# Reworking the front of a fused attention and feed-forward kernel: loads, masks, and the order of the first feed-forward pass

## The chip, the cores and the metric

The kernel runs on one core of one Trainium2 chip. The metric is the device time of one execution in microseconds (us), as a median over several executions. The core has five engines that work side by side (in the kernel before, TensorE is busy for 97% of the span, VectorE for 58, ScalarE for 43 and GpSimd for 24): TensorE (PE in the profile), VectorE (DVE), ScalarE (ACT), GpSimd (POOL) and SyncE (SP), besides 16 DMA engines. "Granted clock" is the TensorE clock that the chip allowed, as a share of full speed; the trace records when it changed. "Span" is the time from the first to the last instruction of the profiled execution, about 1.7 us less than the device time.

## The reference, cut to what matters

```python
# q, k, v: (8 batches, 8 heads, 576 rows, 64) float32
scores = scale * np.matmul(q, k.transpose(0, 1, 3, 2))
mask_plain = (rel >= 0) & (rel < 32)                           # heads 0 to 3
mask_dil = (rel >= 0) & (rel < 128) & (rel % 4 == 0)           # heads 4 to 7
scores = np.where(masks, scores, -1e9)
...                                                            # softmax over the row
attn_out = np.matmul(attn, v)
x = attn_out.transpose(0, 2, 1, 3).reshape(8 * 576, 512)
g = x @ w_gate                                                 # 512 x 1536
out = (gelu(g) * (x @ w_val)) @ w_out                          # 4608 x 512
```

## The kernel before

Heads are worked on in pairs. A batch has four pairs: 0 and 1 with the plain mask, 2 and 3 with the dilated one. The finished pair n goes to tile `xT[n]` (128 features by tokens, float16), and the feed-forward part contracts over these four tiles. The "front" is batch 0's attention, after which the first chunk of 512 tokens can enter the feed-forward part; the attention of later batches is woven into it.

The front, with cuts (`...`). Filler matmuls (`warm`) keep TensorE at work during the first loads. `gate["dma"]` and `gated` make the next load wait until an earlier one has landed.

```python
for t, src, eng in ((0, q, nc.sync), (1, k, nc.scalar)):
    eng.dma_start(out=first_p[:, t], in_=sixes(src, 0))      # both plain pairs, float32
qd0 = load_eights(0)                                         # dilated q, k: cast DMA on GpSimd
...
identity(); mask_plain(); mask_dil()                         # GpSimd selects over whole masks
gate_v = v_plain(0, sv0, nc.sync)
nc.sync.dma_start(out=fh(first_vd), in_=quads(v, 0, HK, 0, 4 * P))   # dilated v, float32
warm(24, 7)
...                                                          # casts, transposes of pairs 0 and 1
gate["dma"] = gate_v
load_w_halves(0)                                             # first third of gate and value weights
v_cast(0, sv0)
emit_s(0, 4, pe_mask=True)                                   # scores and exponentials of pair 0
emit_s(1, 0, pe_mask=True)
t_dil(0, 0, qd0, 4, ("dve", "dve"))
...
w1 = load_w(1)[1]                                            # second third
...
den(3, 4)
norm_x(2, 2)                                                 # xT of pair 2, on DVE
num(3, 0)                                                    # xT of pair 3, on DVE
load_w(2)
gate["dma"] = w1                                             # batch 1's q, k wait for the second third
for t, src in ((0, q), (1, k)):
    gated(nc.sync.dma_start(out=st1[:, t], in_=sixes(src, 1)))
```

The first two feed-forward blocks take the four `xT` tiles one after the other, each tile for all four accumulations before the next, so that TensorE can start with the tile that is ready first:

```python
def ffn1_two(c, pairs, order, split):
    kcs = parts_of(order)
    for group in [kcs[:-1], kcs[-1:]] if split else [[kc] for kc in kcs]:
        for nb in range(2):
            for gi in range(2):
                ffn1_part(c, nb, gi, pairs[nb][gi], group)
...
ffn1_two(c, ..., range(NKC), False)                          # order 0, 1, 2, 3
```

The softmax here doesn't subtract the row's maximum and nothing guards it: scores larger than these inputs give would overflow.

## Time and profile before

| What | Before |
|---|---|
| device time, median of 3 runs | 348.39 us (348.38 to 348.97) |
| span of the profiled execution | 347.0 us |
| TensorE busy | 336.0 us, 97% |
| granted clock | 1.0 throughout the work |
| first feed-forward matmul | 20.97 us |
| its first two blocks done | 25.29 us |
| last transposes for batch 1 start | 43.56 us |
| next feed-forward part starts | 62.06 us |

The lines behind these numbers stand in the prediction. A timeline line reads: start, length, engine, source line, operation, destination and sources by the program's names, shapes, count, and in brackets the idle time of the engine before it with what ended it. The place that absorbs most is the wait for batch 1's k at 41.57.

### The profile page before, as it was taken

To read this page: it belongs to the slowest core of one execution; us is meant where nothing else is said; L and a number is where in the kernel's file an instruction comes from. 1 tells how busy PE (TensorE), PEld (TensorE's weight loads), DVE (VectorE), ACT (ScalarE), POOL (GpSimd) and SP (SyncE) were. 2 spreads that over 40 slices of the span, in tenths; PEclk is the share of its full clock that TensorE was granted. 3 is DMA by queue.
4 is the path that set the end of the run, shared out by engine and by line. 5 is a ranking of instruction groups with operands and counts; after the bars stand their busy time and mean duration, and the time that the engine had idled before them with its cause. 6 is when DMAs were issued, how large, how long until landed. Compare 5 with 4: busy or idle time off the path is not lost.

```text
span 347.0 us, 6006 instructions
## 1 busy us (share of the span) xinstructions
PE 336.0 (97%) x2342; PEld 163.7 (47%) x2342; DVE 201.8 (58%) x309; ACT 148.2 (43%) x220; POOL 84.0 (24%) x123
## 2 busy tenths in 40 slices
PE   8879999999999999999999999999999999999996
PEld 3644454444544445444544454444444444444443
DVE  3784488443794359674878576975498423303320
ACT  1753473535543447336553547336633223223321
POOL 8893304630630540351006300510000000000000
PEclk9999999999999999999999999999999999999999
DMA  8999999999999999898169925991100020020002
GB/s 179 225 201 223 205 200 192 184 147 258 178 107 256 191 152 171 201 162 121 62 159 168 157 73 137 195 126 55 70 0 0 32 91 1 2 91 30 2 30 91
DMA packets 107516, 44.44 MB, mean 128 GB/s; under 512 B 83328, under 2 KB 102912, under 8 KB 107488
## 3 DMA queue, kind: packets, MB, share of 16 engines
q1 hardware_dynamic: 84192, 31.01, 39.2%
q0 software_dynamic: 22752, 12.33, 28.9%
q10 hardware_dynamic: 544, 0.72, 0.8%
q8 instruction: 18, 0.29, 0.4%
q14 instruction: 10, 0.08, 0.1%
HBM read 39.85 MB, written 9.44 MB: 142 GB/s over the span
## 4 chain that ended last, share of the span: by engine, by line
PE 70%; DVE 13%; DMA 10%; issue 3%; ACT 2%; SPq 1%; POOL 1%; DVEq 0%; POOLq 0%; ACTq 0%
PE ps L584 42%; PE ps L618 21%; PE ps L472 4%; DMA st<-in_k_dram 4%; DMA sv<-in_v_dram 3%; DMA wv<-in_moe_w_val_dram 3%; DVE dt L500 2%; DVE dt L533 2%; DVE u_all L607 2%; DVE xT L559 2%; DVE rb L544 2%; DVE P L400 2%; DVE xT L510 1%; PE ps L390 1%; DVE rc L542 1%
## 5 line engine op out<-in xcount | busy, mean ns | idle before, releaser
L607 DVE SCALAR_TENSOR_TENSOR u_all<-g,ps 128x512 f16<-128x512 f16 x108 | 72.8, 684 | 76.7 <-PE ps L584 67.9
L606 ACT ACTIVATE g<-ps 128x512 f16<-128x512 f32 x108 | 63.9, 596 | 123.3 <-PE ps L584 122.8
L584 PE MATMUL ps<-xT,wg 128*128 128x512 f16 x432 | 114.0, 379 | 1.2 <-POOL xT L707 0.7
L584 PE MATMUL ps<-xT,wv 128*128 128x512 f16 x432 | 113.8, 379 | 0.2 <-DVE u_all L607 0.2
L618 PE MATMUL ps<-wo,u_all 128*128 128x512 f16 x420 | 96.9, 380 | 0.2 <-DVE qTd L303 0.2
L584 PEld LDWEIGHTS <-wv 128*128 128x128 f16 x432 | 42.2, 98 | 52.8 <-issue 2.9
L584 PEld LDWEIGHTS <-wg 128*128 128x128 f16 x432 | 41.3, 98 | 48.9 <-issue 1.1
L618 PEld LDWEIGHTS <-u_all 128*128 128x128 f16 x420 | 38.4, 98 | 44.7 <-issue 0.8
L629 ACT ACTIVATE osb<-ps 128x512 f32<-128x512 f32 x33 | 19.7, 597 | 38.8 <-PE ps L618 37.8
L228 POOL CAST qp<-st 128x2048 f16<-128x2048 f32 x6 | 11.4, 1893 | 97.8 <-DMA st<-in_k_dram 64.8
L544 DVE STREAM_TRANSPOSE rb<-rc 128x576 f32<-128x576 f32 (+4 forms) x34 | 25.3, 743 | 1.3
L533 DVE STREAM_TRANSPOSE dt<-ps 128x576 f32<-128x576 f32 x21 | 16.3, 778 | 12.4 <-PE ps L472 12.3
L392 ACT ACTIVATE P<-ps 128x1152 f16<-128x1152 f32 x16 | 18.1, 1130 | 11.8 <-PE ps L390 11.8
L370 ACT ACTIVATE P<-ps 128x960 f16<-128x960 f32 x16 | 15.5, 970 | 11.0 <-PE ps L360 11.0
L559 DVE TENSOR_TENSOR xT<-ps,rb 128x576 f16<-128x576 f32 x16 | 17.9, 1129 | 2.2 <-PE ps L472 1.9
L400 DVE TENSOR_TENSOR P<-P,mask_d 128x1152 f16<-128x1152 f16 x13 | 9.8, 751 | 9.7 <-ACT P L392 9.7
L400 DVE TENSOR_TENSOR P<-P,mask_p 128x1344 f16<-128x1344 f16 x14 | 11.8, 856 | 2.9 <-ACT P L371 2.9
L472 PE MATMUL ps<-P,ones 128*64 128x96 f16 (+5 forms) x174 | 11.3, 244 | 2.1 <-DVE P L400 1.5
L472 PEld LDWEIGHTS <-ones 128*64 128x64 f16 x174 | 7.2, 109 | 11.5 <-issue 8.6
L631 DVE TENSOR_SCALAR osb<-ps 128x512 f32<-128x512 f32 x2 | 1.4, 691 | 18.2 <-PE ps L618 18.2
L255 POOL DMA_DIRECT2D vr<-in_v_dram x16 | 9.9, 632 | 5.3 <-DMA wv<-in_moe_w_val_dram 3.6
L500 DVE STREAM_TRANSPOSE dt<-ps 64x576 f32<-64x576 f32 x14 | 10.9, 781 | 0.4
(88 smaller groups left out, 247.8 us busy)
## 6 DMA issues: line engine op xcount, KB each, us to landing
out_dram<-osb SPq DMA_DIRECT2D x35, 256.0 KB, 2.0
sv<-in_v_dram SPq DMA_DIRECT2D x40, 128.0 KB, 3.3
st<-in_q_dram SPq DMA_DIRECT2D x24, 128.0 KB, 3.1
st<-in_k_dram SPq DMA_DIRECT2D x24, 128.0 KB, 3.1
vd<-in_v_dram POOLq DMA_DIRECT2D x7, 256.0 KB, 6.5
wo<-in_moe_w_out_dram POOLq DMA_DIRECT2D x3, 512.0 KB, 19.7
qd<-in_q_dram POOLq DMA_DIRECT2D x6, 256.0 KB, 5.4
qd<-in_k_dram POOLq DMA_DIRECT2D x6, 256.0 KB, 6.9
```

The costliest lines, as they stand in the source:

```text
L392: nc.scalar.activation(pt, ps[:, b0 : b0 + 4, 0:DW], AF.Exp, bias=0.0, scale=scale)
L400: nc.vector.tensor_tensor(pt, pt, mb, ALU.mult)
L472: nc.tensor.matmul(o, lhs, rhs, start=st, stop=True, skip_group_check=True)
L500: nc.vector.transpose(dt[64 * hl : 64 * hl + 64].rearrange("p b c -> p (b c)"), both_rows(1 - hl, b0, hl))
L533: nc.vector.transpose(dst, den)
L544: nc.vector.transpose(rb[:, 0 : 32 * nb].rearrange("p (b c) -> p b c", c=32), bass.AP(tensor=rc.tensor, offset=rc.offset, ap=[rc.ap[0], [1 ...
L559: nc.vector.tensor_tensor(dst.rearrange("p (i m s) -> p i m s", m=2, s=2), num, rb.rearrange("p (s m i) -> p i m s", s=2, m=2), ALU.mult,)
L584: nc.tensor.matmul(ps[:, bank, :], w[:, kc, ns], xT[kc][:, tok], start=first, stop=end)
L606: nc.scalar.activation(g, ps[:, banks[0], :], AF.Gelu)
L607: nc.vector.scalar_tensor_tensor(u_all[:, nb, :], g, USCALE, ps[:, banks[1], :], ALU.mult, ALU.mult)
L618: nc.tensor.matmul(ps[:, bank, :], u_all[:, fc, tb * P : (tb + 1) * P], wo_t[fc // 4][:, fc % 4, :], start=(fc == 0), stop=(fc == NNB - 1),)
L629: nc.scalar.activation(osb, ps[:, bank, :], AF.Copy, bias=0.0, scale=1.0 / USCALE)
```

## The change

It is meant to shorten the front. Of the plain pairs' q and k, only the first pair's are still loaded as float32; the second pair's and the dilated v come by DMAs that cast (they convert float32 to float16 on the way), issued from GpSimd. One block of each mask is built by GpSimd and the rest copied from it by VectorE. The scores of pair 0 run at once, with VectorE masking them. The fillers fall from 24 to 18, and the first feed-forward pass takes the tiles in the order 2, 0, 1, 3. The core of the diff, with cuts:

```diff
+    def copies(n, w):
+        return bass.AP(tensor=mask_p.tensor, offset=mask_p.offset, ap=[mask_p.ap[0], [0, n], [1, w]])
+    def mask_copies():
+        nc.vector.tensor_copy(mask_p[:, PW:PB].rearrange("p (r c) -> p r c", c=PW), copies(2, PW))
+        nc.vector.tensor_copy(mask_p[:, PB : PB + P], mask_p[:, 0:P])
+        nc.vector.tensor_copy(by_class[:, :, 0:P], copies(2, P))
...
-        eng.dma_start(out=first_p[:, t], in_=sixes(src, 0))
+        eng.dma_start(out=first_p[:, t], in_=sixes(src, 0)[:, 0:2])
+    for t, src in ((0, q), (1, k)):
+        nc.gpsimd.dma_start(out=q6b[:, t], in_=sixes(src, 0)[:, 2:4])
+    identity()
     qd0 = load_eights(0)
+    band(run_p.rearrange("p (r c) -> p r c", r=1), 0, 0)
+    band(rest_p.rearrange("p (r c) -> p r c", r=1), 0, 64)
     sv0 = new_v(0)
-    load_v_dil_rest(0)
-    identity()
-    mask_plain()
-    mask_dil()
+    load_v_dil(0)
+    band(rest_d, 64, 48)
...
-    warm(24, 7)
+    warm(11, 7)
+    for t in range(2):
+        cast_six(("dve", "act")[t], q6a, first_p, t, 0)
+    t_plain(0, q6a, 0, 0, ("act", "dve"))
+    warm(3, 3)
+    mask0 = emit_s(0, 4)
+    mask_copies()
+    warm(4, 3)
...
-    emit_s(0, 4, pe_mask=True)
     emit_s(1, 0, pe_mask=True)
-    t_dil(0, 0, qd0, 4, ("dve", "dve"))
-    t_dil(0, 1, qd0, 6, ("act", "act"))
+    den(0, 2)
+    t_dil(0, 0, qd0, 6, ("act", "act"))
+    t_dil(0, 1, qd0, 2, ("dve", "dve"))
...
-                ffn1_two(c, ((4, 5), (6, 7)) if c == 0 else ((6, 7), (0, 1)), range(NKC), False)
+                ffn1_two(c, *((((4, 5), (6, 7)), (2, 0, 1, 3)) if c == 0 else (((6, 7), (0, 1)), range(NKC))), False)
```

## The prediction

> **What bounds the kernel now.** I read the busy shares first, then the timeline of TensorE, then the chain of waits of the first 45 us, then the DMA throughput of the same stretch, and at last the DMA packets that the trace records.

> ```profile
> PE 336.0 (97%) x2342; PEld 163.7 (47%) x2342; DVE 201.8 (58%) x309; ACT 148.2 (43%) x220; POOL 84.0 (24%) x123
> ```

> TensorE has work in 97% of the span, so a change that leaves its work after the front alone gains only what it takes off the start. The timeline of TensorE in the first 45 us (start, length, line, count, idle before and its releaser):

> ```profile
> 1.53 7.51 PE L658 MATMUL ps<-ones 128*128 128x512 f16 x24 [1.53 <-DVE ones L66]
> 8.88 1.26 PE L314 MATMUL ps<-ident,qp 96*128 96x96 f16 x24
> ...
> 13.40 0.95 PE L332 MATMUL ps<-ident,qd 72*128 72x72 f16 x24 [0.82 <-ACT P L370]
> ...
> 20.97 0.38 PE L584 MATMUL ps<-xT,wg 128*128 128x512 f16 x1 [0.37 <-POOL xT L707]
> ...
> 41.57 0.43 PE L314 MATMUL ps<-ident,qp 96*128 96x96 f16 x6 [0.32 <-POOL qp L301]
> ```

> The front (batch 0's attention) lasts until the feed-forward part starts at 20.97. From 25.29 on, the four groups of the first two blocks done, TensorE runs dense up to 40.83; there it transposes batch 1's q, waits 0.32 us for batch 1's k, and from then on is dense to the end: no later idle in the timeline is over 0.41 us. So whatever the front gains must pass the wait at 41.57. What stands behind it, in the chain of waits of this stretch (start, length, what):

> ```profile
> 3.88 11.30 DMA sv<-in_v_dram
> ...
> 17.74 9.37 DMA wv<-in_moe_w_val_dram
> ...
> 27.55 13.09 DMA st<-in_k_dram
> 40.64 0.05 issue
> 40.69 0.83 POOL qp L301
> 41.52 0.05 issue
> 41.57 0.43 PE ps L314 x6
> ```

> It is a chain of transfers, not of engine work: v of batch 0, then the second third of the gate and value weights (wv lands at 17.74 + 9.37 = 27.11), then batch 1's q and k, which are held back until those weights land, then a cast on GpSimd. Are the transfers late because they are issued late, or because the DMA engines are full? Throughput of 16 to 27 us (40 equal slices):

> ```profile
> DMA  9999999999999999999999999999999999999999
> GB/s 201 205 194 197 246 186 184 184 196 194 194 194 199 199 196 203 201 205 205 201 214 205 201 216 197 209 205 201 205 212 205 209 209 209 197 220 194 209 201 216
> DMA packets 3138, 2.23 MB, mean 203 GB/s; under 512 B 95, under 2 KB 3137, under 8 KB 3137
> ```

> Full throughout. These are cast transfers, counted at their float16 output; 203 GB/s out is about 406 GB/s of float32 read. The packets say the same of the whole start: from 1.75 us on there is no gap, and the last packet of the second weight third starts at about 25.75 us. Up to there the DMA engines move batch 0's q, k, v (3 x 1.18 MB of float32, plus 0.33 MB read twice) and four weight pieces of 1.05 MB: 8.06 MB in 24.0 us, 336 GB/s. **The DMA engines bound the first 41 us; TensorE bounds the rest.**

> [...]while two queues are active, they start packets about one for one (36 cast packets of 1024 B and 36 of 256 B per 0.25 us near 9.5 us). So moving loads from SyncE's queue to GpSimd's buys no bandwidth. [...]The 24 filler matmuls fit: 7.51 us = 11 x 0.427 + 13 x 0.216, the switch at about 6 us. [...]the kTr copy of 128x256 takes 228 ns on DVE and 401 ns on POOL.

> **The change part by part.**

> *First pair of q, k.* Before, 2 x 576 KB of float32 land at 0.81 + 6.9 = 7.7 and 0.81 + 7.5 = 8.3 us. Now half of it. In the packets, the first 384 of the 768 of these loads had started by 4.5 us, and landing trails by about 1 us: 5.4 to 5.8. Cast on DVE 0.58 and on ACT 0.83, 12 transposes 0.6, copies 0.75, 3 fillers 0.65, scores 0.47: scores of pair 0 end near 8.3 (before: 11.1) and its exponentials (0.97 + 0.48) near 9.8 (before 12.5). A gain of 2.7 us for pair 0 alone.

> *Second pair, dilated q, k.* [...]second pair (384 packets), then dilated q, k (576), then v. The first packet of this queue starts at 6.7 us in the trace though it was issued at 1.40, and I take the same start. From there 384 cast packets of 1536 B read (about 61 ns of one engine each, scaled from 80 ns for 2048 B) are 1.5 us, 576 x 80 / 16 = 2.9 us, and the rest of v's 256 B packets beside them 1.3 us: done near 12.4, dilated k landed near 13.5. Before: 2.29 + 11.1 = 13.4. No gain: the dilated pairs still wait for the same bytes.

> *Masks.* POOL's selects and memsets before the weights (0.88 + 0.66 + 2.99 + 0.73 + 1.33 = 6.6 us, from 4.24 to 10.95) shrink to about 2.8 (2 x 0.29 identity, 2 x 0.36 run, 2 x 0.55 rest, 2 x 0.21 dilated rest), with four short memsets and three copies, 0.4 + 0.7 us, on DVE while it is idle (it waited 4.18 us). The weights are issued from about 9.5 instead of 10.97. The DMA engines are full then, so earlier issue alone moves nothing.

> *v dilated as a cast DMA.* 512 KB on SyncE and a POOL cast of 1.07 us go; the same bytes come by GpSimd's queue. TensorE had waited 0.44 us for that cast, but not on the bounding chain.

> *Denominator of pair 0 before the dilated part.* Takes 0.75 + 0.22 + 0.78 = 1.75 us of DVE out of the crowded stretch after 13.5. DVE then has there: copies 1.5, kTr 0.23, three denominators of 1.8, two products of 1.06: 9.3 us from about 14.3, so the last xT group at about 23.6 against 24.4. TensorE takes 0.86 us per group and now starts with xT of pair 2, which I put near 22.5; with that order the first two blocks end between 24.5 and 26 (before 25.29).

> *The sum.* Two times decide, and the later wins. TensorE's own arrival at batch 1's k: 40.83 + 0.42 before, now shifted by -0.8 to +0.6. Batch 1's k: same bytes ahead of it. What gets cheaper is the 384 float32 packets of the second pair: in the trace they ran at 96 to 107 ns instead of 65 ns (from 4.25 us to about 7), some 2.4 us net of the v packets; as casts 1.5 us. Estimate from these: 0.75 us earlier at best, 0 if the slow spell is due to something else. So the cast that TensorE waits for ends 0 to 0.8 us earlier, and after it nothing changes. TensorE's arrival may take part of that back. Expected gain: 0.5 us, so 348.39 - 0.5 = 347.9 us.

> **The rivals.**

> 1. *The whole front gain reaches the end.* If the dilated loads also land earlier (GpSimd's queue starting at 4 us, not 6.7), the feed-forward part could start up to 2 us earlier, and the time would be 346.4. For it: TensorE, DVE and POOL all lose work in the front. Against: the full DMA engines; the second weight third landed at 27.11 for a use at 28.7 to 29.6, a slack of about 2 us, but batch 1's k has none. It would need that k to land 2 us earlier too, at the same byte count.

> 2. *The new order costs.* [...]v's cast has to wait for v, and the kTr copy of pair 2 and the second weight third's issue stand behind it. If v lands at 15.5 instead of 13, pair 2's scores slip by 1.5 to 2 us, the feed-forward part starts later than now, and the time becomes about 349.5. For it: before, v landed at 15.18 and DVE, not POOL, copied these keys. Against: v is now behind only half as much on SyncE's queue, and its 2560 small packets have the engines nearly to themselves from 4.5 to 6.7 us.

> 3. *The clock drops.* Fillers fall from 24 to 18 and TensorE idles between 9 and 14 us for the second pair and the dilated k. [...] Before shows a granted clock of 1.00 in every stretch and idles under 0.9 us.

> **Range and chances.** From rival 1, weighted low, to the cost of rivals 2 and 3 in part: 346.5 to 349.0, which also covers the run-to-run spread of 348.38 to 348.97. Two per cent is 7 us, a third of the whole front; with the DMA engines full that is out of reach, and nothing added costs as much. Faster 0.01, same 0.975, slower 0.015.

> **What would show it.** Scores of pair 0 near 8 us instead of 10.6; dilated transposes still held until about 13.5; DMA at 9 in all slices to 41 us; the second weight third landing between 26 and 27.3; and a longer TensorE wait for the k cast (up to 1.2 us instead of 0.32) if the feed-forward part starts earlier. I am wrong if batch 1's k lands over 1 us earlier or later than 40.64, or if the first two feed-forward blocks end after 26.5. Predicted time: 347.9 us, 346.5 to 349.0.

## The result, and the profile after

The changed kernel took 351.43 us (median of 4 runs, 350.99 to 351.58) against 348.63 us (348.38 to 348.97, 4 runs) of the kernel before in the same rounds. Ratios here are the mean time of one kernel's fast runs over that of the other's of the same rounds, so not quite the ratio of the medians quoted: 1.0078, with a 95% interval of 1.006 to 1.0095. By the 2% rule that is "same", yet it is 2.8 us slower and lies above the predicted range of 346.5 to 349.0. What separates them is the granted clock: 0.995 in all four runs after, 1.0 in the profiled run before, and 0.998 to 1.0 in the runs of the kernel before in all later rounds.

The busy line of the page after:

```profile
PE 335.6 (96%) x2344; PEld 163.2 (47%) x2344; DVE 203.9 (58%) x315; ACT 148.4 (42%) x220; POOL 82.6 (24%) x118
```

TensorE has as much work as before and the span is 2.8 us longer: idle time was added. The timeline of TensorE after, in the front, answers to the one in the prediction:

```profile
7.63 0.47 PE L364 MATMUL ps<-qTp 64*128 64x160 f16 x10 [0.20 <-DVE qTp L297]
...
13.08 0.95 PE L336 MATMUL ps<-ident,qd 72*128 72x72 f16 x24 [1.17 <-DMA qd<-in_k_dram]
...
22.66 0.38 PE L588 MATMUL ps<-xT,wg 128*128 128x512 f16 x1 [2.41 <-DVE xT L563]
22.87 0.42 PE L588 MATMUL ps<-xT,wv 128*128 128x512 f16 x1
23.09 0.63 PE L588 MATMUL ps<-xT,wg 128*128 128x512 f16 x1
...
26.07 0.59 PE L588 MATMUL ps<-xT,wv 128*128 128x512 f16 x1
26.50 0.38 PE L588 MATMUL ps<-xT,wg 128*128 128x512 f16 x1
...
27.79 1.03 PE L588 MATMUL ps<-xT,wg 128*128 128x512 f16 x4
...
43.33 0.68 PE L318 MATMUL ps<-ident,qp 96*128 96x96 f16 x12
```

The scores of pair 0 start at 7.63 instead of 10.64, and the dilated transposes at 13.08 instead of 13.40: the early part works as meant. Then three things stand in the next lines. TensorE waits 2.41 us, for the tile of pair 2. From 23.09 on each matmul takes 0.63 us instead of 0.38 and starts 0.43 us after the last instead of 0.21. And the first two blocks end at 27.79 instead of 25.29. At 43.33 all twelve transposes of batch 1's first pair run as one group, so the wait at 41.57 that bounded the kernel before is gone.

Were the other tiles ready? The timelines of VectorE and GpSimd after, at that time:

```profile
21.52 2.12 DVE L563 TENSOR_TENSOR xT<-ps,rb 128x576 f16<-128x576 f32 x2
```

```profile
19.13 2.76 POOL L719 TENSOR_TENSOR xT<-xT,rb 128x576 f16<-128x576 f32 x2 [3.05 <-ACT xT L718]
```

GpSimd writes `xT` of pairs 0 and 1, done at about 20.5 and 21.9. VectorE writes those of pairs 2 and 3, the first done at about 22.6. The order 2, 0, 1, 3 asks for the one that comes third.

```profile
19.66:23.07 3.41, 0.88 (x14) 0.62 (x14) 3.27 (x6) 1.35 (x2) 3.41 (x4) 1.00 1.24 205
23.07:26.48 3.41, 3.41 (x9) 1.21 (x8) 0.57 (x1) 0.00 (x0) 3.41 (x6) 0.50 1.13 174
```

```profile
19.66:23.07 3.41, 2.71 (x36) 1.66 (x37) 2.92 (x5) 1.46 (x2) 3.41 (x4) 1.00 1.31 204
23.07:26.48 3.41, 3.35 (x16) 1.36 (x14) 2.31 (x4) 1.21 (x3) 3.41 (x5) 1.00 1.24 206
```

In the window before the fall TensorE worked 0.88 us in the changed kernel and 2.71 in the kernel before. The window after it ran at half clock: 9 matmuls instead of 16 for the same full 3.4 us. Half of 3.41 us, 1.7 us, is lost.

The chain of waits after (start, length, what) no longer runs through batch 1's k:

```profile
4.25 8.79 DMA qd<-in_k_dram
...
20.82 0.78 DVE rb L548
21.59 1.02 DVE xT L563
22.62 0.04 issue
22.66 20.84 PE ps L588 x88
```

It goes from the dilated k through VectorE's work on the denominators to the tile of pair 2, and from there on it is TensorE. Before, DMA made up 10% of the chain and now 3%.

A last difference lies in the next stage. The last transposes for batch 1 start at 45.58 (before 43.56, so 2.02 later), but the next feed-forward part starts at 64.93 (before 62.06, 2.87 later): the stage took 19.35 us instead of 18.50. VectorE, GpSimd and TensorE after:

```profile
51.23 1.72 DVE L404 TENSOR_TENSOR P<-P,mask_p 128x1344 f16<-128x1344 f16 x1 [0.81 <-ACT P L375]
...
51.21 1.04 POOL L206 CAST vp<-sv 128x1024 f16<-128x1024 f32 x1 [9.62 <-DMA sv<-in_v_dram]
...
56.22 0.44 PE L476 MATMUL ps<-P,ones 128*64 128x288 f16 x4 [0.70 <-DVE dt L537]
```

and the same product and cast before:

```profile
49.23 0.86 DVE L400 TENSOR_TENSOR P<-P,mask_p 128x1344 f16<-128x1344 f16 x1 [0.66 <-ACT P L371]
...
52.49 1.04 POOL L212 CAST vp<-sv 128x1024 f16<-128x1024 f32 x1 [9.43 <-DMA sv<-in_v_dram]
```

This product of scores and mask takes 0.86 us by itself and 1.72 us where it starts 0.02 us after a GpSimd cast, and TensorE waits 0.70 us for what follows it.

### The profile page after: what moved, and what is told of

Same layout as the page of the kernel before. It is cut to its first block, busy times and chain, and to the rows that moved or that the text cites. A ratio compares the mean times of both kernels' runs of the same rounds, so it can differ in the third digit from the quotient of the medians.

```text
span 349.8 us, 6009 instructions
## 1 busy us (share of the span) xinstructions
PE 335.6 (96%) x2344; PEld 163.2 (47%) x2344; DVE 203.9 (58%) x315; ACT 148.4 (42%) x220; POOL 82.6 (24%) x118
## 4 chain that ended last, share of the span: by engine, by line
PE 76%; DVE 15%; issue 3%; DMA 3%; ACT 2%; POOL 1%; DVEq 0%; POOLq 0%; ACTq 0%
PE ps L588 48%; PE ps L622 21%; PE ps L476 4%; DMA qd<-in_k_dram 3%; DVE dt L537 2%; DVE rb L548 2%; DVE xT L563 2%; DVE dt L504 2%; DVE P L404 2%; DVE u_all L611 2%; DVE xT L514 1%; PE ps L394 1%; DVE rc L546 1%; PE ps L364 1%; PE ps L646 1%
## 5 line engine op out<-in xcount | busy, mean ns | idle before, releaser
L548 DVE STREAM_TRANSPOSE rb<-rc 128x576 f32<-128x576 f32 (+4 forms) x34 | 25.3, 743 | 1.3
L537 DVE STREAM_TRANSPOSE dt<-ps 128x576 f32<-128x576 f32 x23 | 17.9, 779 | 12.6 <-PE ps L476 12.5
L374 ACT ACTIVATE P<-ps 128x960 f16<-128x960 f32 x16 | 15.5, 970 | 12.2 <-PE ps L364 12.1
L404 DVE TENSOR_TENSOR P<-P,mask_p 128x1344 f16<-128x1344 f16 x15 | 13.5, 912 | 3.2 <-ACT P L375 3.2
```

The costliest lines, as they stand in the source:

```text
L404: nc.vector.tensor_tensor(pt, pt, mb, ALU.mult)
L537: nc.vector.transpose(dst, den)
L548: nc.vector.transpose(rb[:, 0 : 32 * nb].rearrange("p (b c) -> p b c", c=32), bass.AP(tensor=rc.tensor, offset=rc.offset, ap=[rc.ap[0], [1 ...
```

## The experiments

The theory: the order makes TensorE wait for pair 2, and the wait leaves too little TensorE work in one window of 3.41 us (0.88 us in after, 2.71 in before), so the clock halves for the next. Rivals: the wait alone costs the time; the front's new loads and masks cost it; the collision of VectorE and GpSimd costs it. Runs called "undisturbed" have a granted clock of 0.998 or more.

### The order and the clock

**e1_order0123**: the changed kernel with the old order.

```diff
-                ffn1_two(c, *((((4, 5), (6, 7)), (2, 0, 1, 3)) if c == 0 else (((6, 7), (0, 1)), range(NKC))), False)
+                ffn1_two(c, ((4, 5), (6, 7)) if c == 0 else ((6, 7), (0, 1)), range(NKC), False)
```

> The changed kernel with the old order (0, 1, 2, 3) of the first two feed-forward blocks, nothing else. Theory A (the order 2, 0, 1, 3 makes TensorE wait 2.4 us for xT of pair 2, and that wait drops the clock): groups start near 20.6, 22.0, 22.7 and 23.7, the two blocks end near 24.6 instead of 27.8, the granted clock stays at 1.0, the DVE mask product near 50 us takes 0.86 us again, and the time is 1.0 to 1.5 us under the kernel before (ratio 0.996 to 0.997). Theory B (fewer fillers or the long wait for the dilated q, k drop the clock): the clock still falls to 0.5 for 3.4 us near 23 us, and at least 1.7 us of the loss stays (ratio 1.003 or more).

Measured: 347.45 us (6 runs), before 348.81; ratio 0.9978 (0.9948 to 1.0007). Five runs lie between 347.31 and 347.63 at clock 1.0 (mean 347.44), one at 350.98 with clock 0.985. TensorE's timeline:

```profile
20.43 0.38 PE L588 MATMUL ps<-xT,wg 128*128 128x512 f16 x1 [0.35 <-POOL xT L719]
...
21.79 0.38 PE L588 MATMUL ps<-xT,wg 128*128 128x512 f16 x1 [0.34 <-POOL xT L719]
...
24.40 1.03 PE L588 MATMUL ps<-xT,wg 128*128 128x512 f16 x4
```

The first block starts at 20.43 with short waits and both end at 24.40, 0.89 us earlier than before and 3.39 us earlier than after. Everything else in the change makes the kernel faster by about 1.4 us when the clock holds; over all six runs the interval still includes 1. One run in six shows that the clock does not always hold.

**e4_before2013**: the kernel before with the new order, and nothing else (the same line exchanged the other way).

> The kernel before with only the order 2, 0, 1, 3 taken over. Theory A: TensorE waits from about 20.5 to 23.4 for xT of pair 2, the clock falls for 3.4 us at about 23.0, the two blocks end near 28.3 instead of 25.3; the wait for batch 1's k (0.32 us) goes; time 2.3 to 3.0 us over the kernel before (ratio 1.0065 to 1.0085), so the order alone makes the whole loss. Theory B (the loads or the masks make it): ratio under 1.003.

Measured: 351.22 us (5 runs), ratio 1.0066 (1.0053 to 1.0079), clock 0.994 or 0.995 in all five. The timeline:

```profile
23.57 0.58 PE L584 MATMUL ps<-xT,wg 128*128 128x512 f16 x1 [2.80 <-DVE xT L559]
...
28.67 1.03 PE L584 MATMUL ps<-xT,wg 128*128 128x512 f16 x4
```

A wait of 2.80 us, a fall of the clock at 23.53 for 3.41 us, and a loss of 2.4 us, without any other part of the change. The order by itself is enough for a loss of this size.

**e2_fill11** and **e3_fill4**: the changed kernel, order kept, with filler matmuls in the wait, to part the wait from the clock.

```diff
     num(3, 0)
+    warm(11, 4)          # e2; e3 has warm(4, 4)
```

> The changed kernel with order 2, 0, 1, 3 kept and 11 filler matmuls put before the first feed-forward matmul. Theory A: the wait for xT of pair 2 stays (first matmul near 22.7), but the clock is held, so the two blocks end near 26.1 instead of 27.8; the DVE mask product near 50 us no longer meets GpSimd's cast of v, so 0.85 us more comes back: time 0 to 0.6 us over the kernel before (ratio 1.000 to 1.002). If the clock is not the matter but only the wait, the time stays at 1.006 to 1.009.

> As with 11 fillers, but only 4 (0.86 us of work): asks how much work in a 3.41 us stretch holds the clock. TensorE then works some 1.7 of the 3.41 us before 23.07, against 0.9 in the changed kernel and 2.7 in the kernel before. If about half is enough, the clock stays at 1.0 and the time is that with 11 fillers; if not, it is that of the changed kernel (ratio about 1.008).

Measured: e2 349.18 us (6 runs), ratio 1.003 (0.9998 to 1.0062). Its five undisturbed runs have a mean of 349.21; one run, the profiled one, took 353.07 with a clock that fell at 13.15 already. e3 349.97 us (4 runs), ratio 1.0042 (1.0019 to 1.0064), three undisturbed at 349.36 to 350.30, the profiled one at 351.74 with a fall at 14.37. So with four fillers the clock held at 23 in these four runs. With the clock held, the order still costs 349.21 - 347.44 = 1.8 us, the wait itself; against the changed kernel's 351.43, from other rounds, what the fillers bring back is about 2.2 us, of which 1.7 is the halved window. Why e3 is half a microsecond over e2 stays open. The undisturbed runs of e2 and e3 have no profile of their own.

### The collision on VectorE

**e5_vcast_act**: batch 1's v cast on ScalarE instead of GpSimd; for room, the output buffers were cut from four to two.

```diff
-    osbp = ctx.enter_context(tc.tile_pool(name="osbp", bufs=4))
+    osbp = ctx.enter_context(tc.tile_pool(name="osbp", bufs=2))
...
-    v_cast(1, sv1)
...
+            v_cast_act(1, sv1)
```

> The changed kernel with batch 1's cast of v taken from GpSimd and given to ScalarE at a later place (the v staging gets two buffers and the output staging two instead of four to make room). Theory A2 (the DVE mask product of 1.72 us at 51.2 was blocked by that cast, and was on the path): the product takes 0.86 us, and the time falls by 0.7 to 0.9 us against the changed kernel, to about 350.6 (ratio to the kernel before about 1.0055). Rival: the product is slow for another reason, or its delay is hidden: it stays at 1.7 us, or the time stays within 0.2 us of the changed kernel (ratio about 1.008).

Measured: 368.1 us (4 runs), ratio 1.0557. A failed design, as TensorE's timeline shows:

```profile
79.45 0.58 PE L596 MATMUL ps<-xT,wg 128*128 128x512 f16 x1 [15.08 <-ACT osb L641]
```

With two output buffers ScalarE waited 21.42 us for the stores, and TensorE 15.08 us for ScalarE. The product did take 0.86 us, but the time says nothing of the collision.

**e5b_vcast_act**: the same cast on ScalarE, the staging buffer put into columns of `xT` that are not used yet, so that the output buffers stay at four.

```diff
-    sv1 = new_v(1)
+    sv1 = x32[2][:, 0 : 5 * HK * D].rearrange("p (k h d) -> p k h d", k=5, h=HK)
+    tiles["v", 1] = vset[1]
-    v_cast(1, sv1)
...
+            v_cast_act(1, sv1)
```

> The experiment on batch 1's cast of v again, without its fault: the first try took two output buffers away, and TensorE then stood 15 us behind the stores. Now only the v staging of batch 1 lies elsewhere (in columns of xT that are not yet in use), and the cast is on ScalarE at a later place. Theory A2: the DVE mask product near 51 us takes 0.86 us instead of 1.72, TensorE's idles before 54 and 56 us shrink by about 0.85 us in sum, and the time is 350.6, 0.7 to 0.9 us under the changed kernel (ratio to the kernel before 1.0045 to 1.006). Rival: the delay of the product is made up elsewhere; the ratio stays at 1.007 to 1.008.

Measured: 352.42 us (6 runs), ratio 1.0116 (1.0093 to 1.014). The product takes 0.86 us and the stage 18.49 (18.50 in before), and yet the time is no lower. In the profiled run the clock fell twice, at 13.24 for 10.24 us and at 26.90 for 3.41 us, and no run was undisturbed. Inconclusive on the time.

**f1_after_fill** and **f2_after_fill_vcast**: the changed kernel with five fillers in the wait for the dilated k (all 11 runs of e8 and f4, below, are undisturbed with them), without and with the cast on ScalarE.

```diff
-    def t_dil(b, hp, q8, b0, engs):
+    def t_dil(b, hp, q8, b0, engs, fill=0):
...
+            if t and fill:
+                warm(fill, b0 + t)
...
-    t_dil(0, 0, qd0, 6, ("act", "act"))
+    t_dil(0, 0, qd0, 6, ("act", "act"), fill=5)
```

> The changed kernel, order 2, 0, 1, 3 kept, with only the 5 fillers in the wait for the dilated k. The drop at 13 or 14 us does not come (no clock under 0.993), the one at about 23 us still does (clock 0.994 to 0.996), time 351.0 to 351.6, ratio 1.007 to 1.009.

> The same with batch 1's cast of v moved from GpSimd to ScalarE. If the stage from the last transposes of batch 1's q, k to the next feed-forward part takes 19.35 us in most runs of the changed kernel, as in its profiled one, and 18.49 without the cast, this is 0.7 to 0.9 us under the kernel with fillers only, at about 350.5 (ratio 1.0050 to 1.0065). If the collision is the accident of single runs, or the order's loss would have grown otherwise, the two are equal within 0.3 us.

Measured: f1 351.82 us (6 runs), ratio 1.0076 (1.0054 to 1.0097); f2 352.18 us (6 runs), ratio 1.0096 (1.0073 to 1.0118). Moving the cast gains nothing here. The clocks were partly missed as well: two runs of each were at 0.989 or 0.99, and one of f1 held 1.0 throughout. That one took 349.78 us; the three of f1 at 0.995 have a mean of 351.47, 1.7 us more, in the same kernel and rounds. The traces show why the cast is not worth its 0.85 us. In f1 the product at 51 us starts just before the cast, and the cast is the one that takes longer, 1.71 instead of 1.04 us; but a later product collides. VectorE, GpSimd and TensorE of f1:

```profile
87.45 2.27 DVE L406 TENSOR_TENSOR P<-P,mask_d 128x1152 f16<-128x1152 f16 x1 [1.45 <-ACT P L398]
...
87.22 1.89 POOL L222 CAST qp<-st 128x2048 f16<-128x2048 f32 x1 [12.57 <-DMA st<-in_k_dram]
...
89.77 0.44 PE L478 MATMUL ps<-P,ones 128*64 128x192 f16 x8 [0.86 <-DVE P L406]
```

This product takes 0.72 us by itself. f2, whose first collision was removed, has the same one there (2.41 us, TensorE idle for 1.00), and so has e2 (2.18 us, idle 0.76). A kernel whose start moved has its products elsewhere against GpSimd's casts, and which of them meet is a matter of that run. None of the profiled runs of before, e1, e3, e4, e6 to e10, f4 and g1 has a product over 0.88 us. Where one is stretched in the stage from batch 1's last transposes, the stage grows with it: 19.35 us in after (1.72 us), 19.36 in f3 (1.58), 18.93 in g2 and g3 (1.15 and 1.29), against 18.48 to 18.58 in all other profiles. From there to the end e2, f1 and f2 take 286.0 to 286.6 us, and all others but e5 284.8 to 285.3. So a collision does cost time in the run that has it. In the profiles f2 had nothing to save in this stage: f1 had no stretched product there either (18.49 us in both), and both lost 1.1 to 1.7 us later.

### Where the front's gain comes from

The prediction said that issuing the weights earlier moves nothing. In e1 SyncE issues batch 1's q at 25.29 us, in before at 27.17. These runs put single parts of the change into the kernel before.

**e6_before_qk**: the second pair's q and k by cast DMA.

```diff
-        eng.dma_start(out=first_p[:, t], in_=sixes(src, 0))
+        eng.dma_start(out=first_p[:, t], in_=sixes(src, 0)[:, 0:2])
+    for t, src in ((0, q), (1, k)):
+        nc.gpsimd.dma_start(out=q6b[:, t], in_=sixes(src, 0)[:, 2:4])
...
```

> The kernel before with only the second pair's q, k as cast DMA on GpSimd's queue. Batch 1's k was issued 1.6 us earlier in the changed kernel (25.6 instead of 27.2). If that came from these 384 float32 packets, which ran slowly (96 to 107 ns each), the second third of the weights lands 1.0 to 1.6 us earlier here; if it came from v or from the shorter work on GpSimd, under 0.5 us. The end: TensorE's wait for batch 1's k shortens, at most 0.3 us, ratio 0.997 to 1.001.

Measured: 348.74 us (4 runs), ratio 1.0003 (0.9987 to 1.002). Batch 1's q is issued at 27.20: no earlier. The expectation missed.

**e7_before_vcastdma**: the dilated v by cast DMA.

```diff
-    load_v_dil_rest(0)
+    load_v_dil(0)
...
-    nc.sync.dma_start(out=fh(first_vd), in_=quads(v, 0, HK, 0, 4 * P))
-    copy("pool", tiles["v", 0][1], r4(first_vd))
```

> The kernel before with only the dilated v as cast DMA (no float32 copy, no cast on GpSimd). If v were the reason why the weights land earlier, they land over 1 us earlier here; I expect under 0.5 us, since the same bytes are read. The second third of the weights is issued where it was, TensorE does not wait 0.44 us for the cast, and the time stays within 0.3 us of the kernel before (ratio 0.999 to 1.001).

Measured: 348.81 us (4 runs), ratio 1.0009 (0.9995 to 1.0024); q issued at 26.99.

**e9_before_masks**: the mask part.

```diff
-    mask_plain()
-    mask_dil()
+    band(run_p.rearrange("p (r c) -> p r c", r=1), 0, 0)
+    band(rest_p.rearrange("p (r c) -> p r c", r=1), 0, 64)
+    band(rest_d, 64, 48)
...
+    mask_copies()
```

> The kernel before with only the mask part of the change (ones by DVE, selects for one block, DVE copies). GpSimd then issues the first weights near 8 to 9 us instead of 11.0. If the early issue is what lets the weights land earlier, batch 1's q is issued at 26.2 or sooner instead of 27.2; if the DMA engines were full anyway, as the prediction said, it stays at 27.0 to 27.2. The time stays within 0.3 us of the kernel before, since TensorE meets batch 1's k in either case (ratio 0.998 to 1.001).

Measured: 348.85 us (4 runs), ratio 1.0015 (0.9995 to 1.0034); one of the four at 350.15 with clock 0.995. GpSimd's timeline:

```profile
9.31 0.78 POOL L146 DMA_DIRECT2D wg<-in_moe_w_gate_dram  x1 [2.67 <-DMA sv<-in_v_dram]
```

GpSimd is done with the masks early and then waits 2.67 us for the landing of v that the first weight load is gated on. The weights are issued 1.66 us earlier than in before, and batch 1's q no earlier (27.36).

**e10_before_masks_qk**: the masks and the second pair's cast DMA together.

> The kernel before with the mask part and the cast DMA of the second pair's q, k together, the order 0, 1, 2, 3 kept. Either alone is expected to give little; if the 1.6 us need both (the cast frees the engines, the early issue fills them), batch 1's q is issued at 25.5 to 26.0 here. If they do not, the rest of it is in the loads of v. Time: TensorE's wait for batch 1's k goes, ratio 0.997 to 1.000.

Measured: 348.38 us (4 runs), ratio 0.9996 (0.9983 to 1.0008). GpSimd's timeline:

```profile
7.98 0.78 POOL L146 DMA_DIRECT2D wg<-in_moe_w_gate_dram  x1
```

The weights go out at 7.98 with no wait for v before them: I read this as v landing earlier, with only half as much float32 ahead of it on SyncE's queue, and the trace agrees: the first piece of v to land took 4.5 us from its issue in e10 and 4.7 in e6, 7.8 in e9 and 8.1 in before. In turn batch 1's q is issued at 25.90 and its k is cast at 39.31 instead of 40.69. TensorE no longer waits for it. The two parts gain 1.27 us of transfer time together and nothing alone: each removes one of two limits on the first weight load (in e6 the masks keep GpSimd until 11.47 and the load goes out at 11.49; in e9 it is v). The time hardly moves, because TensorE's own arrival (its blocks end at 25.11) is now what bounds. These are single profiles, but the 14 with the whole changed front issue batch 1's q between 25.25 and 26.09, so 1.27 us is more than their spread. The remaining 0.6 us of e1's 25.29 was not traced to a part.

### Guarding the clock

**e8_order_fill**, and the same kernel again as **f4_order_fill_again**: e1 with five fillers between the two halves of the first dilated transposes, where TensorE waits for the dilated k. The diff is that of f1 and that of e1 together.

> The changed kernel with the old order 0, 1, 2, 3 and 5 filler matmuls in the 1.1 us in which TensorE waits for the dilated k. In single runs of the kernels with the changed front (1 of 6 with the old order, 1 of 6 and 1 of 4 with fillers before the feed-forward part) the clock fell at 13 or 14 us already, for 7 to 10 us, and cost about 3.5 us. If that wait does it, no run here has a mean clock under 0.998, all runs lie at 347.2 to 347.7 and the ratio is 0.9955 to 0.997 with a narrow interval. If something else does it, a run at 350 or more can still come.

> The same with the 5 fillers in the wait for the dilated k, again. If they guard the clock, no run under 0.998 again (now 12 of 12), and times at 347.4 to 348.0, 0.1 to 0.4 us over the undisturbed runs without them: the fillers end up to 0.2 us after the k has landed. Ratio 0.996 to 0.998, interval under 1.000.

**f3_order_again**: e1 again, beside f4 in the same rounds.

> The changed kernel with the old order, the same kernel again. Runs without a clock drop at 347.3 to 347.6 (0.996 of the kernel before); a run with a drop near 13 us, clock 0.985 to 0.99, at 350 to 351, in about one of five.

Measured: e8 347.85 us (6 runs), ratio 0.9986 (0.9969 to 1.0004); f4 347.78 us (5 runs), ratio 0.9968 (0.9955 to 0.9981); f3 349.38 us (6 runs), ratio 1.0004 (0.9976 to 1.0033). All 11 runs with the fillers are undisturbed; of the 12 without, 5 have a clock of 0.995 or less, 4 of them in f3, far more than the one in five or six that I had expected from e1. In f3's profiled run the clock fell at 17.03, and its timeline has the wait before it:

```profile
17.16 1.12 PE L380 MATMUL ps<-bias_d,ident 128*128 128x288 f16 x4 [1.67 <-DVE dt L537]
```

One of e8's runs took 349.75 at a clock of 0.999. It was not profiled and stays unexplained. f4 is 0.3% faster than the kernel before with an interval that excludes 1, while that of e8, the same kernel, just includes it. So this version beats the changed kernel clearly and the kernel before by 0.7 to 1.0 us in the medians. In f1 and f2, with the order 2, 0, 1, 3, the same fillers did not keep four of twelve runs from a clock of 0.99 or less.

### What sorts the clock windows

In the 20 profiled runs the clock changed only at whole multiples of 3.41 us from its first rise. What sorts the windows of that length that were followed by the half clock ("dropped" below) from those that were not ("held")? I laid eight windows from the first full-clock instant of every profiled run (but e5's) and summed TensorE's work in each. Busy time does not sort them: a window with 1.78 us in e9 held (18.87 to 22.28) and one with 2.22 us in e3 dropped (10.96 to 14.37):

```profile
18.87:22.28 3.41, 1.78 (x39) 1.32 (x35) 1.91 (x4) 2.14 (x3) 3.02 (x3) 1.00 1.36 200
```

```profile
10.96:14.37 3.41, 2.22 (x45) 1.59 (x45) 2.81 (x6) 2.21 (x5) 2.32 (x4) 1.00 1.47 191
```

A sum that does sort them: each matmul's columns at full-clock rate (216 ns per 512), times the share that it uses of the largest form in the traces, 128 by 128 ("the array"). It is my own estimate from shapes and start times in the traces. By it the nine windows that dropped had 0.45 to 1.28 us, and none that held had less than 1.31. The margin is thin: counted again, the figures were 1.30 and 1.32, and they depend on sharing a matmul that crosses an edge between both windows. Counted whole where it starts, the sum no longer sorts all windows: one of g2, below, held with 1.19 and one of e3 dropped with 1.31. Three more runs, variants of e3 with other fillers in the wait for pair 2, were to test this:

```diff
-    warm(4, 4)
+    warm(7, 4, 32, 32)      # g1_small7: 32 rows, 32 columns of the array
+    warm(7, 4, 128, 64)     # g2_half7: 128 rows, 64 columns
+    warm(2, 4)              # g3_fill2: full
```

> The changed kernel with seven filler matmuls of 512 columns in the wait for xT of pair 2, which use only 32 of the 128 rows and 32 of the 128 columns of the array. TensorE is then busy for about 0.9 + 7 x 0.216 = 2.4 us of the 3.41 us window before 23, as long as in windows that held. Theory A (what counts in a window is matmul time weighted by the share of the array in use; the windows so far dropped at up to 1.28 us of it and held from 1.31 us): 0.65 + 1.51/16 = 0.75 us, so the clock is halved at about 23 in every run: granted clock at most 0.995 in all runs, 351.0 to 352.5 us. Theory B (what counts is the time in which TensorE is busy): the clock holds as with four or eleven full fillers: 0.999 or more in most runs, 349.0 to 350.3 us.

> The same with seven fillers of 128 rows and 64 columns, half the array: as busy as with the small ones. Theory A: 0.65 + 1.51/2 = 1.40 us, just over the 1.31 us that held, so the clock holds at 23: 0.999 or more in most runs, 349.0 to 350.3 us. Theory B: the same. With the small fillers the pair tells A from B. If both drop, the weight falls faster than with the share of the array.

> The same with two full fillers in place of seven small ones. Theory A: 0.65 + 0.43 = 1.08 us, under 1.28, so the clock is halved at 23 in every run: at most 0.995, 351.0 to 352.5 us. Theory B: busy for about 1.4 us, and windows that were busy for 1.78 us held while one of 1.88 us dropped, so B says nothing firm, rather a drop. With four fillers (1.51 us by A) the clock held in the undisturbed runs, so this run brackets the limit from below with all else equal.

Measured: g1 350.99 us (4 runs), clocks 1.0, 0.998, 0.995 and 0.985; g2 349.49 us (4 runs), 1.0 in three and 0.99 in one; g3 352.13 us (4 runs), at most 0.995 in all. Their ratios are 1.0062 (1.0003 to 1.0121), 1.0031 (1.0001 to 1.0061) and 1.0095 (1.0059 to 1.0132).

g2 and g3 came out as the weighted sum had it. g1 missed both theories: two of its runs held and two did not. The profiled one held, and shows that my expectation had forgotten the phase. Its first full clock came at 6.90, not 6.00, so its window ran from 20.55 to 23.97 and took in 1.4 us of feed-forward matmuls; by the weighted sum it would hold without any filler. So g1 does not tell the theories apart. What speaks for the weighted sum is that every window of these three traces, none of them used in finding it, falls on its side: those of 0.96 and 1.12 us dropped, and the lowest that held had 1.32 us (0.97, 1.14 and 1.34 when counted again). By busy time one with 2.06 us dropped, more than the 1.78 us that held in e9. It is a good description of these traces, not a proven rule.

## Why the prediction was wrong, point by point

**The step that failed.** It reads: "now starts with xT of pair 2, which I put near 22.5; with that order the first two blocks end between 24.5 and 26". The start was right (22.66). Sixteen matmuls at 0.216 us are 3.46 us, so the blocks would have ended at 26.1 at full clock, on the edge of the stated limit; they ended at 27.79, past the 26.5 that the prediction had named as its sign of being wrong. Two things were missed. I took the start at 22.5 as a fact of VectorE's schedule and never asked what TensorE could do before it, though the trace of before already shows GpSimd's products for tiles 0 and 1 ending at about 22.3, where VectorE's for 2 and 3 only begin:

```profile
19.48 2.79 POOL L707 TENSOR_TENSOR xT<-xT,rb 128x576 f16<-128x576 f32 x2
...
22.26 2.12 DVE L559 TENSOR_TENSOR xT<-ps,rb 128x576 f16<-128x576 f32 x2
```

That wait costs 1.6 to 2.0 us (below). And I had no clock cost at this place.

**Rival 3 had the right event at the wrong place and with the wrong measure.** It looked for a drop of the clock with TensorE idle between 9 and 14 us. There the changed front does come close, and in some profiled runs of its variants drops (e2, e3, e5b, g3). As submitted it drops at 23 in the profiled run; the other three have the same mean clock, 0.995. The measure was an idle time; in the traces the clock changed at multiples of 3.41 us from its first rise, and the fall came with a wait of 2.41 us in after and of 1.67 us in f3. In after it took 1.7 us, half of 3.41, and nothing of that was hidden: the wait at 41.57 was already gone.

**"The later of two times wins" held**, and told the two sides rightly. TensorE's arrival was to shift by -0.8 to +0.6 and shifted by +2.5 (43.33 against 40.83, first transposes), while batch 1's k was cast at 39.22, 1.47 us earlier than before, which was the prediction's other sign of being wrong. So TensorE's arrival won.

**"0 to 0.8 us earlier" for batch 1's k was too small, and "earlier issue alone moves nothing" half right.** Alone it moves nothing (e9), but neither do the cast DMAs (e6); together they gain 1.27 us (e10). The term I had sized, cheaper packets, is not what e6 shows by itself. I had also taken 6.7 us, as before, for the first packet of GpSimd's queue; in the trace after it starts at 4.31, which is the condition that rival 1 named. The dilated k still landed only at 13.04, 0.36 earlier. Rival 1 was therefore nearer the truth for the loads than I allowed: with the old order and a held clock the kernel runs at 347.4. That GpSimd's queue moves its loads one after another was an assumption of mine; it held for the two that matter here: in the trace after, the last packet of the second pair starts at 7.23 us and the first of the dilated q, k at 7.50.

**Rival 2** did not come: the weights' second third was issued at 14.60, earlier than before, and GpSimd's order cost nothing.

**Two readings in the prediction were off, without effect on the sum.** It says that no later idle of TensorE is over 0.41 us; the trace of before has one of 0.61 at 204.57. And two active queues did not always start packets about one for one: near 9.5 us they did (37 on GpSimd's and 36 on SyncE's from 9.375 to 9.625), but from 7 to 8 us it is 64 and 430. That the move to GpSimd's queue gains nothing by itself is what e6 shows (27.20 against 27.17). The switch of the fillers, at about 6 us in the prediction, is at 5.93 in the clock record, 4.4 us after the first filler (1.53); the 20 profiles have 2.9 to 6.0, with full clock at 4.40 us in e7 and at 7.54 in e3.

**Not foreseen:** the collision of VectorE's product with GpSimd's cast. In after the product took 1.72 us instead of 0.86 beside the cast, and in f1 the cast, coming second, 1.71 instead of 1.04.

The account can be made from three profiles. e1 differs from the changed kernel by the order alone, g1 by its seven small fillers alone; in its profiled run (348.92 us) g1 has the new order and a clock of 1.0:

```profile
26.01 1.03 PE L588 MATMUL ps<-xT,wg 128*128 128x512 f16 x4
```

The blocks end at 24.40 in e1, 26.01 in g1 and 27.79 in after: 1.6 us for the wait and 1.8 for the halved window (half of 3.41 is 1.7, and the start was 0.10 later). The collision adds 0.86 (19.35 against 18.49 in e1). Together they are 4.25 us; the profiled runs of e1 and after are 347.31 and 351.55, 4.24 apart. The rest of the change had brought 1.4 (e1, undisturbed, against before), so about 2.9 should be lost, and 2.80 was measured. Runs without a profile agree on the wait: 1.8 us (e2 against e1), and 2.0 for the one run of f1 at clock 1.0 against f4's median. How often the collision strikes in runs that were not profiled is not known.

The range was too narrow because I treated the order of the first pass as free to choose. The 0.975 for a change within 2% stands: the loss is 0.8%.

## What to carry to other kernels

Before reordering work on the engine that bounds, put the ready time of every input beside its new place: an order that asks first for the input that comes third turns the others' readiness into idle time (2.41 us here). When a change takes work away from TensorE, look in the trace at its work in each window of the clock, 3.41 us long here, rather than at the longest idle time: in these profiles the half clock came after waits of 1.67 us (f3), 2.41 (after) and 2.80 (e4), and after windows in which TensorE was busy for 0.65 (e4) to 2.22 of 3.41 us (e3), while one with 1.78 held (e9). Five fillers in a wait cost some 0.3 us here (347.8 against 347.4 undisturbed) and, with the old order, held the clock in all 11 runs. And test the parts of a compound change together as well as alone, since two of them may each remove only one of two limits.
